# Batch 0's two first products lead, the interleaved streams begin one chunk earlier, and loads of k and v wait for the transposes of k

## Chip, cores and metric

One core of a Trainium2 chip. The metric is the device time of one launch in microseconds (us), lower is better. The profiled span runs from the first to the last instruction of one execution; in these runs it is about 1.8 us less than the launch's own time. Runs come with a state, fast or slow; everything below compares fast runs. The granted clock of a stretch is the share of TensorE's full clock that the profile shows as granted there; the landing of a transfer is the time from its issue until its data is in place; PSUM is the memory that matmuls write to, cut into banks.

## The reference, cut to what matters

```python
# B=8, H=8, S=1024, D=64, KP=64; 8192 tokens, d_model 512, d_ff 2048
k_proj = einsum('ks,bhsd->bhkd', E, k)
v_proj = einsum('ks,bhsd->bhkd', F, v)
scores = (q @ k_proj.T) / sqrt(64)
attn   = exp(scores - max) / sum          # softmax over 64 columns
x      = (attn @ v_proj)  -> 8192 x 512   # heads side by side
h      = maximum(x @ w_in, 0)             # the "first" product, 8192 x 2048
out    = (h * h) @ w_out                  # the "second" product, 8192 x 512
```

## The kernel before

The work is cut into 16 chunks: batch b, half c, 512 tokens each. A chunk's x comes out of attention as `xT`, and then has a first and a second product. Each product is done in one of two ways. **Plain**: 64 matmuls of 512 columns. **Seven**: the operands are cut into 2 by 2 blocks and seven half-size products of sums of blocks take the place of eight (112 matmuls of 256 columns; VectorE makes the sums). Most chunks run in "streams": firsts and seconds, both as seven products, alternate in quanta of four matmuls, 28 steps for a chunk. The attention of later batches is put between the quanta by a plan of step numbers.

```python
def first_plain(self, order=..., sums=True):
    for n, fb in enumerate(order):
        ps = bank()
        for cb in range(NCB):
            self.first_mm(fb, cb, ps)         # 4 matmuls of 512 columns
        self.square(fb, ps)                   # ScalarE relu, VectorE square
        if sums and n % HF == HF - 1:
            self.sum_h(n // HF)
        yield                                 # one step of the plan
# ... second_cold: the plain second product, two banks at a time
# ... second_seven: the same by seven products

def project(self):
    ps = att_psum()[:, 0]
    for i in range(NI):
        f, l = i == 0, i == NI - 1
        nc.tensor.matmul(ps[LO, :], lhsT=ET[:, i, :], rhs=self.K[:, :, i, :], start=f, stop=l)
        nc.tensor.matmul(ps[HI, :], lhsT=FT[:, i, :], rhs=self.V[:, :, i, :], start=f, stop=l)
    # ... copies of k by VectorE, of v by ScalarE and VectorE

def transpose_k_dma(self):
    nc.sync.dma_start_transpose(kT, kp)       # views cut

# weights: four pieces of w_out are loaded last
for j in range(WP):
    if j == WP - 1:
        load(Q0[:, :, 4:8, :], tokens(q, 0, i=slice(4, 8)))   # q of batch 0, second chunk
    # ... load of w_out piece j

# the kernel's start: TensorE is kept busy on zeros while loads arrive
warm(8)
ET = projection("ET", e_bf)
warm(4)
# ... attention of batch 0, first chunk, with warm(1) to warm(3) between

# the order of the products before the streams
run_all(chunk[0, 0].first_cold(), chunk[0, 0].second_cold(), chunk[0, 1].first_plain(),
        chunk[0, 1].second_seven(*(bank()[:] for _ in range(3))))
# ...
run_all(chunk[1, 0].first_plain())
# then the streams: firsts from (1, 1) on, seconds from (1, 0) on
#   with, once a batch, at steps counted by t:
    on(t + 2, b + 2, "transpose_q_dma")
    on(t + 11, b + 3, "load_q", ...)
    on(t + 28, b + 2, "project")
    on(t + 30, b + 2, "transpose_k_dma")
    on(t + 32, b + 3, "load_kv")              # straight behind the transpose
```

The softmax here doesn't subtract the row's maximum and nothing guards it: scores larger than these inputs give would overflow.

## Time and profile before

| | before |
|---|---|
| three runs, us | 479.88, 480.07, 483.85 (median 480.07) |
| profiled span, us (same run timed 480.92) | 479.1 |
| granted TensorE clock | 1.0 |
| TensorE busy / weight loads busy | 98% / 73% |
| VectorE / ScalarE busy | 73% / 60% |
| start of the streams, us | 109.48 |

TensorE is busy all through, so the time is the sum of its columns and its gaps. The lines that show this stand in the prediction. This is TensorE's timeline of the kernel before (start, length, engine, line, operation, tiles, shape, count, and in brackets the idle time before and what ended it):

```profile
6.16 1.89 PE L221 MATMUL ps_bank<-zeros 128*128 128x512 bf16 x4
7.98 1.84 PE L272 MATMUL ps_bank<-K_sb,ET 128*64 128x256 bf16 x8
...
25.12 0.38 PE L494 MATMUL ps_bank<-xT,w_in 128*128 128x512 bf16 x1 [0.16 <-issue]
25.76 0.59 PE L494 MATMUL ps_bank<-xT,w_in 128*128 128x512 bf16 x2 [0.26 <-DVE xT L439]
```

The matmul at 25.76 us is the first one after the last piece of the first chunk's `xT`: from here on TensorE runs freely. I call this moment **the start**, and the span less the start **the rest**: 479.1 - 25.76 = 453.3 us before.

### The profile page before, as it was taken

The page shows a single profiled execution, that of the slowest core. Times are in us where ns is not written, and L with a number is a line of the kernel's source. Part 1 is how long each engine was busy: PE and PEld are TensorE (multiplying, and loading weights), DVE is VectorE, ACT ScalarE, POOL GpSimd, SP SyncE. Part 2 cuts the span into 40 slices and gives each one's busy share as a digit, 9 for nine tenths or more (in the row PEclk, how much of TensorE's full clock was granted, in tenths as well). Part 3 has the DMA queues.
Part 4 walks back from the last instruction along what each step waited for, and adds up shares of the span by engine and source line. Part 5 has one row for each costly group of instructions (what it writes and reads, how often), then busy time and mean ns, then how long its engine had stood idle before and what let it go on. Part 6 is the DMA issues. An engine that isn't in the chain of part 4 may idle for free.

```text
span 479.1 us, 10022 instructions
## 1 busy us (share of the span) xinstructions
PE 469.1 (98%) x4096; PEld 351.9 (73%) x4106; DVE 349.2 (73%) x613; ACT 286.2 (60%) x466; POOL 33.3 (7%) x45
## 2 busy tenths in 40 slices
PE   8999999999999999999999999999999999999996
PEld 3444445637878787887878878787878788888885
DVE  2356898856996679767897579966797678967671
ACT  2564567397547774678546785477736775565641
POOL 7410020200010000100010000100000000000000
PEclk9999999999999999999999999999999999999999
DMA  9999998899949497867949498595911054101012
GB/s 180 204 206 206 227 157 158 158 227 207 178 90 181 111 201 175 127 127 185 185 99 204 89 221 176 93 163 135 212 52 55 23 133 112 67 23 67 24 66 89
DMA packets 80046, 66.98 MB, mean 140 GB/s; under 512 B 30720, under 2 KB 76032, under 8 KB 80000
## 3 DMA queue, kind: packets, MB, share of 16 engines
q0 software_dynamic: 30640, 29.23, 39.3%
q1 hardware_dynamic: 49216, 36.97, 29.8%
q8 instruction: 32, 0.52, 0.5%
q10 hardware_dynamic: 144, 0.13, 0.1%
q14 instruction: 14, 0.11, 0.1%
HBM read 59.24 MB, written 16.78 MB: 159 GB/s over the span
## 4 chain that ended last, share of the span: by engine, by line
PE 86%; DVE 8%; ACT 3%; issue 1%; DMA 1%; DVEq 0%; ACTq 0%
PE ps_bank L657 35%; PE ps_second L577 33%; PE ps_bank L494 6%; PE ps_att L334 2%; PE ps_att L263 2%; PE ps_second L554 2%; PE ps_att L410 2%; DVE rs L378 1%; DVE w_in_sum L155 1%; DVE w_out_sum L155 1%; DVE xT L439 1%; DVE h L155 1%; PE ps_bank L221 1%; DMA e_f<-in_E_dram 1%; ACT h L490 1%
## 5 line engine op out<-in xcount | busy, mean ns | idle before, releaser
L155 DVE TENSOR_TENSOR h<-h 128x1024 bf16<-128x1024 bf16 (+1 forms) x182 | 107.8, 615 | 38.9 <-ACT h L667 25.3
L657 PE MATMUL ps_bank<-x_sum,w_in_sum 128*128 128x256 bf16 x624 | 94.0, 273 | 0.0
L657 PEld LDWEIGHTS <-w_in_sum 128*128 128x128 bf16 x832 | 78.7, 98 | 16.2 <-issue 7.5
L577 PEld LDWEIGHTS <-h 128*128 128x128 bf16 x832 | 81.3, 98 | 10.7 <-issue 1.0
L549 ACT COPY u<-ps_bank 128x512 f32<-128x512 f32 x107 | 63.2, 591 | 24.5 <-PE ps_bank L657 21.4
L671 DVE CUSTOM_DVE_ANT_0 h<-ps_bank,u 128x512 bf16<-128x512 f32 x104 | 68.3, 684 | 13.0 <-PE ps_bank L657 12.5
L682 ACT COPY ps_bank<-ps_bank 128x512 f32<-128x512 f32 x52 | 29.7, 570 | 78.7 <-PE ps_bank L657 78.7
L667 ACT ACTIVATE h<-ps_bank 128x512 bf16<-128x512 f32 x104 | 63.0, 606 | 16.4 <-PE ps_bank L657 15.5
L657 PEld LDWEIGHTS <-w_in 128*128 128x128 bf16 x624 | 58.8, 98 | 13.9 <-issue 7.2
L577 PEld LDWEIGHTS <-s 128*128 128x128 bf16 x624 | 61.0, 98 | 7.1
L657 PE MATMUL ps_bank<-xT,w_in 128*128 128x256 bf16 x416 | 62.6, 273 | 0.0
L577 PE MATMUL ps_second<-w_out_sum,s 128*128 128x256 bf16 x416 | 62.5, 273 | 0.0
L577 PE MATMUL ps_second<-w_out_sum,h 128*128 128x256 bf16 x416 | 62.2, 273 | 0.0
L577 PE MATMUL ps_second<-w_out,h 128*128 128x256 bf16 x416 | 60.1, 272 | 0.1
L414 DVE TENSOR_TENSOR xT<-ps_att,rs 128x512 bf16<-128x512 f32 x56 | 36.0, 684 | 15.9 <-PE ps_att L410 15.9
L494 PE MATMUL ps_bank<-xT,w_in 128*128 128x512 bf16 x186 | 44.6, 379 | 2.1 <-DVE xT L439 1.0
L490 ACT ACTIVATE h<-ps_bank 128x512 bf16<-128x512 f32 x48 | 28.1, 606 | 16.1 <-PE ps_bank L494 15.9
L155 DVE TENSOR_TENSOR o_sb<-ps_second,u 128x512 f32<-128x512 f32 x27 | 18.5, 684 | 25.9 <-PE ps_second L577 20.7
L494 PEld LDWEIGHTS <-w_in 128*128 128x128 bf16 x192 | 17.7, 97 | 24.6 <-issue 6.1
L348 ACT ACTIVATE expT<-ps_att 128x1024 bf16<-128x1024 f32 x32 | 32.9, 1036 | 2.9 <-PE ps_att L334 2.5
L657 PE MATMUL ps_bank<-x_sum,w_in 128*128 128x256 bf16 x208 | 31.3, 273 | 0.0
L657 PE MATMUL ps_bank<-xT,w_in_sum 128*128 128x256 bf16 x208 | 31.3, 273 | 0.0
(104 smaller groups left out, 477.8 us busy)
## 6 DMA issues: line engine op xcount, KB each, us to landing
out_dram<-o_sb SPq DMA_DIRECT2D x63, 256.0 KB, 3.1
rs<-inv SPq DMA_DIRECT2D x96, 128.0 KB, 2.6
K_sb<-in_k_dram POOLq DMA_DIRECT2D x7, 1024.0 KB, 10.7
V_sb<-in_v_dram POOLq DMA_DIRECT2D x7, 1024.0 KB, 17.1
Q_sb<-in_q_dram POOLq DMA_DIRECT2D x7, 1024.0 KB, 12.1
w_out<-in_moe_w_out_dram POOLq DMA_DIRECT2D x4, 512.0 KB, 18.0
w_in<-in_moe_w_in_dram POOLq DMA_DIRECT2D x3, 512.0 KB, 14.9
k_f<-in_k_dram SPq DMA_DIRECT2D x1, 512.0 KB, 4.7
```

Source lines behind the costliest of these rows:

```text
L155: return nc.vector.tensor_tensor(out=o, in0=x, in1=y, op=op)
L263: nc.tensor.matmul(ps[LO, :], lhsT=ET[:, i, :], rhs=self.K[:, :, i, :], start=f, stop=l)
L348: self.done = nc.scalar.activation(e[:], ps[:], AF.Exp, scale=SCALE)
L414: self.done = nc.vector.tensor_tensor(out=self.xT[:, pr, :, par], in0=ps_x[par].rearrange("p (c t) -> p c t", c=2), in1=rs[:, par].rearran ...
L490: nc.scalar.activation(h, ps.rearrange("p (a t) -> p a t", a=2), AF.Relu)
L494: nc.tensor.matmul(ps[:], lhsT=w_in_blk(cb, fb), rhs=self.xT[:, cb, self.c].rearrange("p a t -> p (a t)"), start=(cb == 0), stop=(cb == NC ...
L549: nc.scalar.copy(u[:], ps)
L577: nc.tensor.matmul(ps[:, i * HM:(i + 1) * HM], lhsT=self.h_form(n, fb)[:, i * P:(i + 1) * P], rhs=w_out_form(n, fb), start=fresh and i == ...
L657: nc.tensor.matmul(ps[:, j * HC:(j + 1) * HC], lhsT=w_in_form(n, cb, 2 * self.g + j), rhs=self.chunk.x_form(n, cb), start=fresh and j == 0 ...
L667: nc.scalar.activation(self.out(kh, a), ps[:], AF.Relu)
L671: nc.vector._custom_dve(TENSOR_ADD_SAT, out=self.out(kh, a), in0=ps[:], in1=more[:], s0=3.0e38, s1=0.0)
L682: nc.scalar.copy(self.chain[:], self.first[:])
```

## The change

Its intent: batch 0's two first products lead, so the second product of chunk (0,0) can be done as seven products instead of plainly, and so can the first product of (1,0), which moves into the streams. The attention of batch 0's second chunk and of batch 1 is squeezed in earlier, in half chunks. Six squares go to ScalarE. Loads of k and v wait until the DMA transpose of k has landed. k and v are projected to two PSUM banks. Cut to its core (a new plan of steps, buffer counts and re-timed operand sums, and two copies of transposes that move to ScalarE, are cut; `t` is 28 steps larger after than before for the same `b`, since the streams begin one chunk, 28 steps, earlier):

```diff
-    if j == WP - 1:                                  # before the last w_out piece
-        load(Q0[:, :, 4:8, :], tokens(q, 0, i=slice(4, 8)))
+    if j == 2:                                       # after w_in piece 3 of 5
+        for g in range(2):
+            load(Q0[:, half[g], 4:8, :], tokens(q, 0, h=half[g], i=slice(4, 8)))
...
-            ps = att_psum()[:, 0]
+            ps = att_psum()
-  matmul(ps[LO, :], lhsT=ET ...);  matmul(ps[HI, :], lhsT=FT ...)
+  matmul(ps[LO, 0], lhsT=ET ...);  matmul(ps[HI, 1], lhsT=FT ...)
...
-run_all(chunk[0, 0].first_cold(), chunk[0, 0].second_cold(), chunk[0, 1].first_plain(),
-        chunk[0, 1].second_seven(...))
+run_all(chunk[0, 0].first_cold(),
+        chunk[0, 1].first_plain(sums=False, on_scalar=(1, 4, 7, 10, 12, 14)))
...
-run_all(chunk[1, 0].first_plain())
+run_all(chunk[0, 0].second_seven(*banks))
...                                                   # firsts(): (1, 0) is no longer skipped
-            on(t + 2, b + 2, "transpose_q_dma")
+            on(t + (26 if b else 32), b + 2, "transpose_q_dma")
-            on(t + 32, b + 3, "load_kv")
+            on(t + (32 if b else 37), b + 3, "load_kv", lambda b=b: atts[b + 2].kT_done)
```

## The prediction

> **What bounds the kernel now.** I read the page first (busy shares, then the 40 slices), then TensorE's timeline, the waits by stretch, the DMA queue, and VectorE's and ScalarE's timelines between 15 and 112 us. The page:
>
> ```profile
> PE 469.1 (98%) x4096; PEld 351.9 (73%) x4106; DVE 349.2 (73%) x613; ACT 286.2 (60%) x466; POOL 33.3 (7%) x45
> ...
> PE   8999999999999999999999999999999999999996
> ...
> PEclk9999999999999999999999999999999999999999
> ```
>
> TensorE is busy from end to end at full clock; no other engine passes 73%. So the time is TensorE's columns plus its gaps, and a change gains only by taking matmuls or gaps away. Two rates, from TensorE's timeline (start, length, engine, line, tiles, count, and in brackets the idle time before):
>
> ```profile
> 37.17 4.48 PE L500 MATMUL ps_bank<-w_out,h 128*128 128x512 bf16 x20
> 41.49 1.06 PE L309 MATMUL ps_bank<-ident,Q_sb 128*128 128x128 bf16 x16
> 42.38 1.89 PE L500 MATMUL ps_bank<-w_out,h 128*128 128x512 bf16 x8
> ...
> 118.35 0.41 PE L410 MATMUL ps_att<-expT,vp 64*64 64x512 bf16 x4
> 118.69 0.61 PE L657 MATMUL ps_bank<-x_sum,w_in_sum 128*128 128x256 bf16 x4
> 119.14 0.60 PE L577 MATMUL ps_second<-w_out_sum,s 128*128 128x256 bf16 x4
> ```
>
> Start to start, 20 wide matmuls (512 columns) take 41.49 - 37.17 = 4.32 us, 0.216 each; 16 transposes 0.89 us. Later in that timeline a quantum of four 256-column matmuls starts every 0.437 us (18 of them from 119.14 to 127.00), so 0.1092 each. A group of attention matmuls put between costs 0.43 us: the quantum before 118.35 started at 117.82, should end at 118.26, and the next starts at 118.69. A projection of k and v costs 1.94 (135.32 to 137.26).
>
> Where are the gaps? From 112 to 470 us the waits name nothing for TensorE but weight loads of 0.2 to 0.4 us ("issue"), the transitions that I have counted. In 25 to 112 us they name small ones:
>
> ```profile
> PE ps_bank L554 <- DVE h L155: 0.5, 1, 0.5
> PE ps_bank L494 <- DVE qT L323: 0.3, 1, 0.3
> PE ps_bank L494 <- DVE xT L439: 0.3, 1, 0.3
> ```
>
> All waits of matmuls there sum to about 2 us. The start of the kernel to 25.76 us (last piece of the first xT) is not touched, and the streams from 109.48 us run without a gap. The change can act only between.
>
> **What the Trainium skill says.** "TensorE: Matmul & The Clock Gate", Back-to-back issue gap, gives N/2.4 + 2.5 ns for an isolated warm matmul: 215.8 and 109.2 ns for 512 and 256 columns. The trace agrees (216 and 109). The same place gives about 131 ns as the sustained spacing at 512 columns; this trace does not. "Perfetto Trace Analysis", Identifying the Most-Contended Engine, says matmul busy share is a poor measure of headroom and names weight-load share (73% here) instead. Taken here, headroom is in the number of columns, and that is what the change cuts. "PSUM — Partial Sum Buffer", PSUM bank collisions, says different quadrants of one bank may be accessed at the same time. k lies in partitions 0 to 63 and v in 64 to 127 of one bank before, yet ScalarE's copy of v waited for VectorE's copies of k (0.4 us in two cases), so that wait is one of ordering; separate banks may lift it, off TensorE's path. "DMA: Bandwidth & Descriptors", Queues, rings and completion order, says each DMA engine takes turns between queues by packet. The k transposes took 10.1 us to land in the median, 2.3 at the least, the last one, which has no loads of k and v issued beside it. That agrees with sharing.
>
> **The change part by part.**
>
> (a) Two plain products become seven-product ones: the second product of batch 0's chunk 0, and the first product of batch 1's chunk 0. By the instruction order of both programs, 128 wide matmuls go (192 + 64 to 128) and 224 of 256 columns come (112 in each stream). 128 x 0.216 = 27.65 us out, 224 x 0.1092 = 24.46 in: **-3.2 us**.
>
> (b) Attention is cut into chunk halves for batch 1 as for batch 0, so two pairs no longer share one packed group of sums. By both programs' orders: six more groups of sums for one half each, three packed ones fewer, scores and values in the same number of groups: +3 at 0.43 us, less 0.3 for batch 2's k transposes going to DMA: **+1.0 us**. With (a): -2.2.
>
> Both together by stretch. Before, 25.76 to 109.48 us holds 181 wide matmuls (39.1), the 64 wide second ones (13.8), 112 of 256 (12.2), and 15.2 of attention: 80.4 of 83.7 us, so 3.3 us of gaps. After, from 25.76 to the streams: 117 wide (25.3), 112 of 256 (12.2), 10.8 of attention (six transposes of q at 0.45, five groups each of scores and sums, four of values, one projection 1.94, k transposes): 48.3, so the streams start at 74.1 us plus gaps. Their first 28 steps are new: 28 x 0.873 + 8 groups x 0.43 + 1.94 = 29.8. From step 28 on the plan equals the old one from its step 0, with one more group: 479.1 - 109.5 + 0.4 = 370.0. Sum: **474.0 us plus gaps**, against 479.1 with 3.3 of gaps before. So at equal gaps about -1.8 us (0.4 from the count above: groups that stand beside each other before).
>
> (c) Gaps after. I walked the engines' orders by hand with the trace's durations (ACT relu 0.49 back to back, exp or ln 0.95, DVE square 0.34, copy or sum 0.6, xT 0.63). *Loads:* the queue moves about 206 GB/s (bf16 side) there, 2.55 us for 512 KB:
>
> ```profile
> 21.95 0.75 POOL L89 DMA_DIRECT2D w_out<-in_moe_w_out_dram  x1 [1.44 <-DMA V_sb<-in_v_dram]
> 24.73 0.88 POOL L89 DMA_DIRECT2D K_sb<-in_k_dram  x1 [2.03 <-DMA w_in<-in_moe_w_in_dram]
> 27.25 0.87 POOL L89 DMA_DIRECT2D V_sb<-in_v_dram  x1 [1.63 <-PE ps_bank L494]
> ```
>
> The second line says that w_in's blocks 4 to 7 landed at about 24.7. After, q's halves follow (26.0, 27.3), then blocks 8 to 11 (29.9), 12 to 15 (32.4). TensorE reaches q's halves at 28.4 and 29.8 and block 8 at 31.8: it fits by 2 us. k and v of batch 1 land by about 53, their projection comes at about 57. *Start of the second chunk:* batch 0's chunk-1 attention is squeezed into steps 6 to 14. ScalarE runs exp, ln, exp between relus, and VectorE's last xT comes at about 42.0 where TensorE would want it at 41.2: a gap of **0.8 us**. *Chunk (0,1):* VectorE has 16.9 us of squares, s sums and weight sums to do; w_out's sums end at about 57, product 5 wants them at about 59. ScalarE takes six squares and stays under the matmuls' pace (22 x 0.5 = 11 of 13.8 us). *Second product of (0,0):* exp and ln fill ScalarE almost wholly (10.6 of about 10.5 us in steps 7 to 14), and scores, sums and values hand two PSUM pairs round: a few waits of 0.1 to 0.3, **about 1 us**. *First ten stream steps:* ScalarE still works off exp of 1/sum while the bank copies of the streams begin: **0.5 to 1 us**. The k transposes of batch 2 have 9 steps to their scores, some 10.6 us from the start of the projection; the copies take about 5, and with loads held back the transpose should take 2.3 to 5. It just fits. Gaps: about 2.5 to 3, so span 474.0 + 2.8 = 476.8.
>
> (d) Holding loads of k and v behind the transposes costs nothing later: the next projection is over 40 us away, a load takes 5 us at the rate above. The separate banks cost and save nothing on TensorE. The change of the h and x_sum buffers (nine shared) moves one x_sum to just before its use; VectorE has room.
>
> **Rivals.** *First: nothing is lost on the way, and the denser order removes the old gaps too.* For it: the old waits of matmuls stem from sums and copies that are moved. Against: the work of ScalarE and VectorE per us of matmul rises in 25 to 75 us. It would give 474 to 475. *Second: a new wait in the thick part takes back the 1.8 us and more.* Candidates: ScalarE, where before one four-us stretch already ran nearly full (4.72 of 5 us in 45 to 50); q or w_in landing late, if 1 KB runs of q move slower than my rate; the k transposes of batch 2 against their nine steps, where every us of delay is a us of time. For it: three margins of about 2 us each. Against: none falls short by the sums above. It would give 479 to 485. *Third: the gain is larger in the steady part, because transposes land earlier.* Against: TensorE has no wait on kT from 112 us on (transposes issued at 140.45 landed about 150.8, scores ran at 151.51). It would give nothing.
>
> **Range and chances.** The measured time before is 1 us over the profiled span (480.07 and 479.1), so 476.8 + 0.9 = 477.7; I round to 477.5. Low end 474 (gaps near zero), high end 482 (one of the three margins fails by 3 to 4 us). Over 2% faster means under 470.5, less than TensorE's bare columns by my sum: 0.02. Over 2% slower means above 489.7, at least 12 us of new gaps: 0.04, for a transfer that collides in a way I did not see. Within 2%: 0.94.
>
> **What would show it.** In TensorE's timeline after: start of the streams at 75 to 78 us (my sum 74.1 plus gaps of 1 to 3); first part to 25.76 us the same; 28 steps later about 30 us on; then the same 55.5 us for each batch. Waits of matmuls should name xT at the second chunk's start (near 41 us), ScalarE's copies or exp between 58 and 85 us. The k transposes' median landing should fall from 10.1 to under 5 us. I am wrong if a wait on kT, qT, w_in or q of over 2 us stands in TensorE's list, if a batch in the streams takes more or less than 55.5 us by 0.5, or if the streams start before 74 us.

## The result, and the profile after

| | before | after |
|---|---|---|
| median, us (four runs each) | 479.99 (479.88 to 483.85) | 475.57 (475.43 to 475.9) |
| ratio of fast runs, 95% interval | | 0.989 [0.984, 0.9939]: within 2% |
| profiled span, us (own time) | 479.1 (480.92) | 473.7 (475.5) |
| granted clock | 1.0 | 1.0 |
| start / rest, us | 25.76 / 453.3 | 24.04 / 449.7 |

A ratio here is the mean time of one kernel's fast runs over that of the other's of the same rounds, so it is not quite the ratio of the medians quoted. The page of the changed kernel:

```profile
PE 465.2 (98%) x4224; PEld 361.3 (76%) x4230; DVE 348.3 (74%) x606; ACT 296.1 (63%) x482; POOL 33.9 (7%) x47
...
PE   8899999999999999999999999999999999999996
...
PEclk9999999999999999999999999999999999999999
```

There are 128 more matmul records on TensorE, but 3.9 us less busy time (469.1 to 465.2), at the same clock. TensorE is still the bound. Its timeline at the start, and where the parts of the change begin:

```profile
5.80 1.04 PE L222 MATMUL ps_bank<-zeros 128*128 128x512 bf16 x4
7.07 1.03 PE L278 MATMUL ps_bank<-K_sb,ET 128*64 128x256 bf16 x8 [0.23 <-ACT K_sb L726]
...
37.30 2.33 PE L504 MATMUL ps_bank<-xT,w_in 128*128 128x512 bf16 x9
39.81 0.38 PE L504 MATMUL ps_bank<-xT,w_in 128*128 128x512 bf16 x1 [0.17 <-DVE xT L446]
40.41 13.33 PE L504 MATMUL ps_bank<-xT,w_in 128*128 128x512 bf16 x60 [0.22 <-DVE xT L446]
53.57 1.91 PE L564 MATMUL ps_bank<-w_out,h 128*128 128x256 bf16 x16
...
73.45 0.60 PE L667 MATMUL ps_bank<-xT,w_in 128*128 128x256 bf16 x4
...
102.66 0.60 PE L667 MATMUL ps_bank<-xT,w_in 128*128 128x256 bf16 x4
```

The first two lines are the same work as the first two of the timeline before: there four wide matmuls on zeros took 1.89 us (with the 128x256 ones, 1.84, still half as fast), here 1.04. The clock was open by about 6 us here, and at about 9.5 us before. The other lines are the landmarks. The second chunk starts at 37.30 (two of its 72 wide matmuls, up to 53.57, have no record here); two small waits for `xT` at 39.8 and 40.4; the second product of (0,0) as seven products starts at 53.57; the streams start at 73.45; 28 steps later it is 102.66. The whole list of waits of TensorE's matmuls from 24 us to the end is one line (us in total, times, longest; one of the three, 0.26 us, ends at the start itself):

```profile
PE ps_bank L504 <- DVE xT L446: 0.7, 3, 0.3
```

And the transposes of k by DMA, before (first fence) and after (second), the view of the tile `kT`:

```profile
L300 SPq DMA_TRANSPOSE kT<-kp x5: 1210/1269/1336, 140.5 to 362.6; - x5
...
DMA to landing us min/median/max: 2.3/10.1/10.3
```

```profile
L306 SPq DMA_TRANSPOSE kT<-kp x6: 1195/1203/1233, 85.3 to 357.2; - x6
...
DMA to landing us min/median/max: 2.3/2.3/2.9
```

The median landing falls from 10.1 to 2.3 us, once no load of k and v is issued beside it.

**Where the 5.4 us of span came from.** The start is 1.72 us earlier, and the rest is 3.6 us shorter. The rest can be added up from the landmarks. The bare work is the prediction's count; that of the remainder is the same stretch as measured in the kernel before, plus one group, so its gap is only a difference to that kernel.

| stretch after | measured, us | bare work, us | gaps, us |
|---|---|---|---|
| start to streams | 73.45 - 24.04 = 49.41 | 48.3 | 1.1 |
| first 28 steps | 102.66 - 73.45 = 29.21 | 29.8 - 0.87 = 28.9 | 0.3 |
| the remainder | 473.7 - 102.66 = 371.04 | 370.0 + 0.87 = 370.9 | 0.2 |
| sum | 449.7 | 448.1 | 1.55 |

The 0.87 are two quanta of 0.437 us that I had put among the first 28 steps and that fall after them, because step 0 has no second product yet and the first group's last product comes late. The bare work before was 80.4 us up to the streams and 479.1 - 109.48 = 369.6 from there, 450.0 in all, with 3.3 of gaps. So the bare work fell by 1.9 and the gaps by 1.75. The gaps are what the count leaves over, so an error of the count would stand in them. The lists of waits say about the same: after the start they name 2.0 us before (2.3 from 25 us on, less the 0.26 that end at 25.76) and 0.4 after, 1.6 less.

### The profile page after: what moved, and what is told of

It reads as the page before. It is cut to its first block, busy times and chain, and to the rows that moved or that the text cites.

```text
span 473.7 us, 10305 instructions
## 1 busy us (share of the span) xinstructions
PE 465.2 (98%) x4224; PEld 361.3 (76%) x4230; DVE 348.3 (74%) x606; ACT 296.1 (63%) x482; POOL 33.9 (7%) x47
## 4 chain that ended last, share of the span: by engine, by line
PE 89%; DVE 4%; DMA 3%; ACT 2%; SPq 1%; issue 1%; DVEq 0%; ACTq 0%
PE ps_bank L667 35%; PE ps_second L587 34%; PE ps_bank L504 4%; PE ps_bank L564 3%; PE ps_att L269 2%; PE ps_att L341 2%; PE ps_second L564 2%; DMA rs<-inv 2%; PE ps_att L417 2%; DMA k_f<-in_k_dram 1%; PE ps_att L394 1%; DVE xT L446 1%; PE ps_bank L316 1%; DVE h L156 1%; DVE xT L421 1%
## 5 line engine op out<-in xcount | busy, mean ns | idle before, releaser
L667 PE MATMUL ps_bank<-x_sum,w_in_sum 128*128 128x256 bf16 x672 | 101.2, 273 | 0.0
L667 PEld LDWEIGHTS <-w_in_sum 128*128 128x128 bf16 x896 | 84.3, 98 | 18.8 <-issue 9.6
L587 PEld LDWEIGHTS <-h 128*128 128x128 bf16 x896 | 87.6, 98 | 11.4 <-issue 1.1
L681 DVE CUSTOM_DVE_ANT_0 h<-ps_bank,u 128x512 bf16<-128x512 f32 x112 | 73.9, 685 | 16.9 <-PE ps_bank L667 12.7
L559 ACT COPY u<-ps_bank 128x512 f32<-128x512 f32 x115 | 68.0, 591 | 25.5 <-PE ps_bank L667 24.0
L677 ACT ACTIVATE h<-ps_bank 128x512 bf16<-128x512 f32 x112 | 67.9, 607 | 16.7 <-PE ps_bank L667 15.8
L667 PE MATMUL ps_bank<-xT,w_in 128*128 128x256 bf16 x448 | 67.4, 273 | 0.0
L421 DVE TENSOR_TENSOR xT<-ps_att,rs 128x512 bf16<-128x512 f32 x48 | 30.9, 685 | 14.1 <-PE ps_att L417 14.1
L587 PE MATMUL ps_second<-w_out,s 128*128 128x256 bf16 x224 | 33.6, 273 | 0.0
L504 PE MATMUL ps_bank<-xT,w_in 128*128 128x512 bf16 x124 | 29.9, 379 | 1.8 <-DVE xT L446 1.5
L504 PEld LDWEIGHTS <-w_in 128*128 128x128 bf16 x128 | 11.8, 98 | 16.8 <-issue 4.4
## 6 DMA issues: line engine op xcount, KB each, us to landing
K_sb<-in_k_dram POOLq DMA_DIRECT2D x7, 1024.0 KB, 10.3
Q_sb<-in_q_dram POOLq DMA_DIRECT2D x6, 1024.0 KB, 11.8
```

The lines of the kernel that those rows point to most:

```text
L421: self.done = nc.vector.tensor_tensor(out=self.xT[:, pr, :, par], in0=ps_x[par].rearrange("p (c t) -> p c t", c=2), in1=rs[:, par].rearran ...
L504: nc.tensor.matmul(ps[:], lhsT=w_in_blk(cb, fb), rhs=self.xT[:, cb, self.c].rearrange("p a t -> p (a t)"), start=(cb == 0), stop=(cb == NC ...
L559: nc.scalar.copy(u[:], ps)
L587: nc.tensor.matmul(ps[:, i * HM:(i + 1) * HM], lhsT=self.h_form(n, fb)[:, i * P:(i + 1) * P], rhs=w_out_form(n, fb), start=fresh and i == ...
L667: nc.tensor.matmul(ps[:, j * HC:(j + 1) * HC], lhsT=w_in_form(n, cb, 2 * self.g + j), rhs=self.chunk.x_form(n, cb), start=fresh and j == 0 ...
L677: nc.scalar.activation(self.out(kh, a), ps[:], AF.Relu)
```

## The experiments

Twelve runs in three groups, each on one chip with its own runs of the kernel before. Where a difference of less than one us matters, I compare the rest of one profile with that of another, because the time itself contains the start, which varies (see a_again). The rest of a given kernel repeats within about 0.6 us: 453.3, 453.9 and 453.5 for the kernel before, 449.7, 449.9 and 449.5 for the changed one (the last of each with a longer warm-up).

### 1. a_again: the changed kernel, unaltered

> The changed kernel unaltered, as the control of this group. Of the 5.4 us between the two profiled spans, 1.7 lie ahead of the first matmul of the first xT (25.76 against 24.04 us), which the change does not touch. If that is the phase of TensorE's clock warming up, this profile may show a start anywhere between 24 and 26 us, and the time stays near 475.6 us. If the change itself makes the start shorter, the start is again at 24.0.

Measured: median 477.51 us (477.07 to 479.43), ratio 0.9945 [0.9928, 0.9963]: half the gain of the first result has gone. TensorE's timeline:

```profile
5.83 1.89 PE L222 MATMUL ps_bank<-zeros 128*128 128x512 bf16 x4
7.65 1.87 PE L278 MATMUL ps_bank<-K_sb,ET 128*64 128x256 bf16 x8
...
25.46 0.81 PE L504 MATMUL ps_bank<-xT,w_in 128*128 128x512 bf16 x3 [0.26 <-DVE xT L446]
...
74.87 0.60 PE L667 MATMUL ps_bank<-xT,w_in 128*128 128x256 bf16 x4
```

Here the zeros take 1.89 us as in the kernel before, and the start is at 25.46, not 24.04. The span is 475.4, so the rest is 449.9. The rest is a property of the kernel, the start is not: the same kernel, same code, gave 24.04 and 25.46. "TensorE: Matmul & The Clock Gate" of the Trainium skill, Part 1, says that the clock gate watches a free-running window of about 3.4 us and that the number of cold matmuls therefore varies from run to run; the traces agree in that the number varies: four wide matmuls took 1.04 us at 5.80 and 1.89 at 5.83, at about half the rate. The window itself shows in no run here.

### 2. b_again: the kernel before, unaltered

> The kernel before, unaltered, for a second profile of its start. If the start of 25.76 us is one of two phases of the clock's warm-up, this one may show 24 to 26; if the kernel before always starts late, 25.8 again. Time 480 us either way.

Measured: 480.56 us (479.36 to 481.61), ratio 1.0011 [0.999, 1.0032]; start 25.85, span 479.7, rest 453.9. The kernel before repeats as well; it merely starts late in both profiles.

### 3. e8_warm10_after and e9_warm10_before: a longer warm-up in both

```diff
-        warm(8)
+        warm(10)
         ET = projection("ET", e_bf)
```

> The changed kernel with ten in place of eight matmuls on zeros at the very start, which fill the gap of 0.4 to 0.7 us ahead of the first transposes. Over ten profiles, the start (first matmul after the last xT) lay between 24.0 and 26.2 us for the same instructions, the late ones with half-speed matmuls until about 9.5 us. Theory: the gap decides whether TensorE's clock opens at 5 or 9.5 us. Then the start is 24.0 to 24.8 in every run, the median 475 and the spread under 1 us (it was 477.07 to 479.43 in one group and 475.43 to 475.9 in another). Rival (the late start is the loads): median and spread as before, 475.5 to 479.

> The kernel before with the same ten matmuls. Theory: 0.5 to 1.5 us faster than the kernel before, 478.5 to 479.3, and from the start to the end still 453.6 us. Against the changed kernel with ten it then shows what the change itself is worth without the luck of the clock: 3.8 us.

Measured in one group: e8 475.44 us (475.17 to 476.59), ratio 0.9898 [0.988, 0.9916], start 23.86, rest 449.5; e9 479.96 us (479.51 to 480.21), ratio 0.9988 [0.9972, 1.0003], start 24.34, rest 453.5. The kernel before ran from 479.44 to 481.63 in this group, 2.2 us wide; e9 is 0.7 wide. The medians differ by 4.5 us; of the 4.4 between the two profiled spans, 0.5 is the start and 3.9 the rest. With the start nearly alike in the two profiles, **the change is worth about 4 us**. The half us was there before the first projection began (6.90 and 7.35 us): from there to the start it takes 16.96 us in e8, 16.99 in e9 and 16.97 in the first profile of the changed kernel, so the change itself does not shorten the start. The three profiles with ten matmuls on zeros (e8, e9, e10) start at 23.86 to 24.34, the eleven with eight at 24.03 to 26.21; that fits the theory, but three profiles do not prove it. Not all was met: e8's start lay under its 24.0 and its spread was 1.4 us, not under 1, and e9's median lay above its 479.3. Whether the longer warm-up gains time is not shown: e9 is like its kernel within the noise, and no unaltered run of the changed kernel stands in this group (475.44 here, 475.57 and 477.51 in others).

### 4. e1_one_bank: v projected to the bank of k again

```diff
-                nc.tensor.matmul(ps[HI, 1], lhsT=FT[:, i, :], rhs=self.V[:, :, i, :], start=f, stop=l)
+                nc.tensor.matmul(ps[HI, 0], lhsT=FT[:, i, :], rhs=self.V[:, :, i, :], start=f, stop=l)
...
-            self.keep_v(ps[HI, 1])
+            self.keep_v(ps[HI, 0])
```

> k and v projected to one PSUM bank again, all else as changed. My theory (the gain is columns of TensorE and fewer gaps): no difference to the changed kernel, under 0.3 us. Rival (separate banks save a wait of TensorE or of the k copies): 1 us or more slower.

Measured: 475.85 us, ratio 0.991 [0.9893, 0.9927]; rest 449.6 against 449.9 of a_again on the same chip. The separate banks are worth nothing on the time. (Its median is 1.7 us under a_again's with nothing better in the rest. Its profiled start was 24.82 against 25.46; there the clock opened early, but TensorE waited 1.01 us for ScalarE's copy of the first k, and in e4 0.52 us for a load of k, so a late operand can move the start too. ScalarE's copy of v still waits for VectorE's copies of k, 1.2 us in five cases with two banks and 1.1 with one, so the banks do not lift that wait either. For the other runs only the times are known.)

### 5. e3_plain_second: the second product of (0,0) plain again

```diff
-        at(18, chunk[0, 0].sum_h, 0)
-        at(20, chunk[0, 0].sum_h, 1)
...
-        run_all(chunk[0, 0].second_seven(*banks))
+        run_all(chunk[0, 0].second_plain(banks))   # 4 token blocks, 16 wide matmuls each
```

> The second product of batch 0, chunk 0 is done plainly again (64 wide matmuls in place of 112 of 256 columns), in 16 steps at the same place. My theory: 64 x 0.216 - 112 x 0.1092 = 1.6 us slower than the changed kernel, perhaps up to 0.3 less since VectorE is spared eight sums. Rival (columns are not what counts, the gaps are): no slower, since VectorE has 4.8 us less to do.

Measured: 478.44 us, ratio 0.9957 [0.9942, 0.9973]; rest 451.2, so +1.3 against a_again. TensorE's timeline:

```profile
38.63 15.83 PE L504 MATMUL ps_bank<-xT,w_in 128*128 128x512 bf16 x72
54.30 1.03 PE L510 MATMUL ps_bank<-w_out,h 128*128 128x512 bf16 x4
...
76.61 0.60 PE L676 MATMUL ps_bank<-xT,w_in 128*128 128x256 bf16 x4 [0.67 <-ACT o_sb L517]
```

From the product's start to the streams it takes 76.61 - 54.30 = 22.31 us; in a_again 74.87 - 54.98 = 19.89. Of the 2.42 us, 0.67 is a wait for a copy of the result that the experiment itself brings in. The other 1.75 fits 64 x 0.216 - 112 x 0.1092 = 1.6: the gain of columns for one product stands at the place where it was expected. The rest grew by 1.3 only, because e3 saves about 0.6 us before this stretch and 0.5 after it (a_again has a wait of 0.4 there for a second-product bank). As to the first of these, the small waits for `xT` at the second chunk's start are gone: 72 matmuls in one run from 38.63, most likely because VectorE was spared the sums of h for (0,0), the only work that this edit takes from it there.

### 6. e4_q_late: the second half of batch 0's q loaded late again

```diff
-        if j == 2:
-            for g in range(2): load(Q0[:, half[g], 4:8, :], ...)
...
+        if j == WP - 1:            # before the last piece of w_out
+            for g in range(2): load(Q0[:, half[g], 4:8, :], ...)
```

> The second half of batch 0's q is loaded behind three quarters of w_out, where the kernel before had it, all else as changed. My theory: it lands near 39.6 us as it did before, TensorE wants it at 26.8, so 12 to 13 us of wait, plus up to 2 us of slow clock after it: 12 to 15 us slower than the changed kernel. Rival (order of loads does not matter, the queue has room): under 2 us.

Measured: 489.67 us (487.93 to 490.09), ratio 1.0193 [1.0173, 1.0214]; rest 463.5, +13.5 to 13.9 against the three profiles of the changed kernel. TensorE's timeline:

```profile
38.20 1.03 PE L316 MATMUL ps_bank<-ident,Q_sb 128*128 128x128 bf16 x8 [10.43 <-DMA Q_sb<-in_q_dram]
39.03 1.91 PE L504 MATMUL ps_bank<-xT,w_in 128*128 128x512 bf16 x4
```

A wait of 10.43 us, and after it four wide matmuls in 1.91 us, where they take 1.03 at full clock. The granted clock over the stretches (start and end; width, then busy time and count of each engine, the clock, the DMA share, GB/s):

```profile
27.00:37.00 10.00, 0.77 (x4) 0.15 (x2) 1.12 (x3) 1.39 (x3) 1.76 (x2) 0.77 1.27 204
37.00:41.00 4.00, 2.80 (x15) 1.70 (x16) 1.02 (x2) 0.02 (x1) 0.00 (x0) 0.50 1.31 204
41.00:60.00 19.00, 18.61 (x116) 7.64 (x114) 14.48 (x32) 16.13 (x25) 1.75 (x2) 0.96 1.05 163
```

By stretches of one us, the clock fell to 0.50 during the wait, between 32 and 33 us, and rose again between 42 and 43. So TensorE worked some 4.4 us, from 38.2 to about 42.6, at half rate, which loses about 2.2. Two later waits for ScalarE, of 1.0 us (a logarithm, explained under e7) and 0.2, complete the sum: 10.4 + 2.2 + 1.2 = 13.8. Moving this load is what makes the new order possible; it is not a gain but a condition.

### 7. e2_loads_free: k and v loaded without waiting for the transpose

```diff
-  on(t + (32 if b else 37), b + 3, "load_kv", lambda b=b: atts[b + 2].kT_done)
+  on(t + (32 if b else 37), b + 3, "load_kv")
```

> Loads of k and v no longer wait for the transposes of k. My theory: the k transposes land 10.3 us after issue in place of 2.3, so batch 2's, issued at 85.3, lands at 95.6 and its scores, at 91.4 us now, wait about 4.2 us; later batches have 16 steps and lose under 0.5 in all: 4 to 5 us slower than the changed kernel. Rival (the transposes were late for another cause): landing stays at 2.3, no difference.

Measured: seven runs from 485.74 to 503.46 us, median 492.37; ratio of the fast runs 1.019 [1.015, 1.0231]. Three of the seven, the profiled one among them (503.46 us, clock 0.98), were classed slow, by their times against the fastest of this kernel. No other kernel here spreads as wide (17.7 us), so the class may have taken up part of the effect itself. Four fast runs have a mean of 489.6, against 477.8 for a_again in the group: **+12 us, where I expected 4 to 5**. In the profile, TensorE's waits and the landing of `kT`:

```profile
PE ps_att L341 <- DMA kT<-kp: 17.7, 4, 6.1
```

```profile
DMA to landing us min/median/max: 2.4/13.4/15.5
```

And its timeline at the longest wait:

```profile
99.72 0.64 PE L341 MATMUL ps_att<-qT,kT 64*64 64x512 bf16 x4 [6.12 <-DMA kT<-kp]
100.30 1.04 PE L667 MATMUL ps_bank<-x_sum,w_in_sum 128*128 128x256 bf16 x4
101.12 1.06 PE L587 MATMUL ps_second<-w_out_sum,h 128*128 128x256 bf16 x4
```

Two things were missed. The landing got worse than in the kernel before (13.4 against 10.1), so four batches waited and not one. And after such a wait quanta that take 0.60 us take 1.04; the granted clock from 100 to 104 us was 0.58. The sizes of single waits come from a profile classed slow and are not those of the fast runs; that it costs over 10 us not to hold the loads, with everything else as changed, the fast runs show alone.

### 8. e7_free_q_early: loads free, and the transposes and loads of q at their old steps

```diff
-  on(t + (26 if b else 32), b + 2, "transpose_q_dma")
+  on(t + (2 if b else 32), b + 2, "transpose_q_dma")
...                                  # load_q of batch b + 3 back at t + 11; e2's edit kept
```

> As e2 (loads of k and v free), and from batch 3 on the transposes and loads of q are back where the kernel before had them, 24 steps earlier than the transposes of k. e2 lost far more than I expected: its k transposes landed after 13.4 us in the median, not 10.3, and four batches waited. Theory: the q transposes issued just ahead on the same queue add the missing 3 us. Then landing falls to about 10.3 from batch 3 on, only batch 2 waits (some 6 us and 2 to 3 of slow clock after it): 8 to 10 us slower than the changed kernel, some 485. Rival (something else makes the landing long): 13 us still, as slow as e2, some 492.

Measured: 480.13 us (479.83 to 482.42), ratio 1.0002 [0.9981, 1.0024]; rest 452.5. The view of `kT` and the waits of TensorE's matmuls:

```profile
DMA to landing us min/median/max: 2.3/9.9/10.0
```

```profile
PE ps_att L417 <- ACT inv L398: 2.9, 1, 2.9
```

The landing goes back from 13.4 to 9.9, the 10.1 of the kernel before. So the excess of e2 comes from the transposes of q that the change puts four steps ahead of those of k, on the same queue; the 10 us come from the loads. (This run moves the loads of q with them. But in e2 itself, beside loads, the four k transposes that took 11.8 to 15.5 us were issued while the q transpose was still in flight, as at 145.4 us with q landing at 148.7; the one at 206.5, issued after q had landed at 205.3, took 10.3.) No matmul waits for `kT` any more. I expected about 485 because I thought batch 2 would still wait. It did not: batch 3's loads of k and v came only at 89.6 us, behind a load of q, and the transpose was issued at 86.8, so that it could land in the 2.3 us that it takes alone. The loss in the rest against the changed kernel (2.8 us; of the 4.7 us in time against e8 a further 1.8 is the start, 25.71 against 23.86) is one wait for a logarithm on ScalarE, which itself sat idle until 113.33 us. The profile names a store of the output as what it waited for, but another transfer fits better. By the code the logarithm writes a buffer from a pool of three, which one `inv` and two `rs` tiles take in turn, so the copies `rs<-inv` out of the `inv` before must have landed first. The last of these was issued at 106.6 and took 6.7 us, so it landed at 113.3. In the changed kernel the last was issued at 105.4, took 2.8 us, and nothing waited. The shorter waits of the same name in e4 (1.0 us) and e10 (0.5 us) end in the same way: the last copies were issued at 118.4 and 104.7 and took 4.8 and 4.3, and the logarithms started at 123.2 and 109.1. What was slow in e7 is likely the queue: its edit brings a load of q from 114.9 to 88.8 us, ahead of those of k and v, and the load of v lands 22.3 us after its issue instead of 14.3. So the loads need not be held as such: with the transposes of q early, letting them go cost this one wait in the profile.

### 9. e5_dve_squares: all squares of (0,1) on VectorE

```diff
-  chunk[0, 1].first_plain(sums=False, on_scalar=(1, 4, 7, 10, 12, 14))
+  chunk[0, 1].first_plain(sums=False, on_scalar=())
```

> All squares of batch 0, chunk 1 on VectorE again. It gets 6 x 0.34 = 2.0 us more in a stretch where it runs without a break from 38 to 57 us. w_out's first sums then end 1.5 us later, still before product 5 (57.3 us), and the copies of k end at 60.9 where TensorE transposes k at 60.3: 0.3 to 1 us slower. Rival (VectorE has room there): no difference; second rival (VectorE is the bound there): 2 us slower.

Measured: 476.31 us, ratio 0.9925 [0.9906, 0.9943]; rest 450.4, +0.5 to 0.9. The waits of its matmuls are those of a_again (1.0 us for `xT`, 0.4 for ScalarE's copy of a second-product bank), so none of them is put down to the squares; the difference is as large as the spread of the rest between runs of one kernel. The six squares on ScalarE are worth under 1 us, and that they are worth anything is not shown.

### 10. e6_two_banks_first: the second chunk's first matmuls spread over two banks

```diff
+            ahead = {}
+            if on_scalar:                       # only (0, 1)
+                for fb in order[:2]:
+                    ahead[fb] = bank()
+                    for cb in range(2):         # column blocks whose xT is there
+                        self.first_mm(fb, cb, ahead[fb])
             for n, fb in enumerate(order):
-                ps = bank()
-                for cb in range(NCB):
+                ps = ahead[fb] if fb in ahead else bank()
+                for cb in range(2 if fb in ahead else 0, NCB):
```

> A try to beat both: the second chunk of batch 0 begins with the first two blocks of xT for two output banks, so that its third and fourth block are wanted 0.43 us later each. The gaps at 39.2 to 40.4 us are 0.95 us in the trace of the changed kernel. My theory: most of it goes, 0.6 to 0.9 us faster. Rival (the gap moves on to the next wait): no difference.

Measured: 475.24 us (474.85 to 477.46), ratio 0.9911 [0.989, 0.9931]; rest 449.5, 0.2 under the changed kernel's. TensorE's timeline:

```profile
37.30 15.99 PE L504 MATMUL ps_bank<-xT,w_in 128*128 128x512 bf16 x72
53.13 1.91 PE L570 MATMUL ps_bank<-w_out,h 128*128 128x256 bf16 x16
```

The second product starts at 53.13 instead of 53.57, from the same 37.30: 0.44 us saved. At the end 0.2 is left, with a wait of 0.4 us for ScalarE's copy of a second-product bank, which a_again has too and the first profile of the changed kernel has not. The expected 0.6 to 0.9 did not come.

### 11. e10_both: two banks first and the longer warm-up

This is e6's edit and e8's together, the version that might beat both kernels.

> Ten matmuls at the start and two banks first at the second chunk, a try at a version that beats both. From the start to the end 449.3 us as in the run with two banks first; time 474.5 us, 0.3 us under the changed kernel with ten. Rival: no gain beyond the warm start.

Measured: 475.31 us (474.77 to 475.74), ratio 0.9892 [0.9873, 0.9911]; rest 449.7, with a wait of 0.5 us for ScalarE's logarithm. It is not better than e8 (475.44 in the same group) or the changed kernel beyond the noise. No version here beats the change.

## Why the prediction was right, and which terms were not

The range held: 475.57 lies between 474 and 482, 1.9 us under the 477.5. The repeat of the same kernel, a_again, came to 477.51; that this hits the middle value is luck, since two errors cancel in it (below). The mechanism was right; the sizes, step by step:

- **Columns, -3.2 us: right.** Of the two products the one that could be undone alone (e3) gave 1.75 us where half the sum, 1.6, was expected. The other, the first product of (1,0), was not undone; its half stands on the count.
- **Attention in half chunks, +1.0 us: consistent, not shown alone.** Bare work after adds up to 448.1 us with it, and 1.55 us of gaps fill the measured 449.7.
- **Gaps, 2.8 us: the term that was mis-sized.** Measured 1.55 us, a little over half. By place: the start of the second chunk was right in place, releaser and size. It has 53.57 - 37.30 - 72 x 0.216 = 0.7 us against 0.8, by `xT` on VectorE, at 39.8 and 40.4 us. The second product of (0,0) was to have about 1 us of waits for ScalarE and PSUM pairs; no such wait stands in the list, and what is left of the stretch's 1.1 us is 0.4. The first steps of the streams were to have 0.5 to 1; they have 0.3. In both places I had called out ScalarE as nearly full, and in the first profile of the changed kernel no matmul waited for it; a_again has a single such wait, of 0.4 us, and it is in the streams. The first rival (denser order, no new gaps, 474 to 475) came nearer; the third, a gain in the steady part, gave nothing, as the prediction had argued: the remainder differs by 0.2.
- **The start, "not touched": wrong as a statement about a run.** The instructions there are the same in effect, yet the start moved from 25.76 to 24.04 because the clock opened earlier, and the rest of the kernel moved with it. It is chance as far as the change goes: 25.46 in a_again, 23.86 to 26.2 over all profiles. So of the first result's 5.4 us of span, 1.7 are not the change's. For the same reason one test that I set failed by its letter: the streams began at 73.45, before 74 us. Counted from the start, 49.4 us was measured and 74.1 - 25.76 + 2 = 50.3 to be expected with 2 us of gaps.
- **From span to time, +0.9 us: mis-sized.** I took a median of runs less the span of another run. The profiled run itself took 480.92, 1.8 us over its span. The two errors of the middle value go opposite ways: 1.8 for 0.9 raises it, while 1.25 us fewer gaps and a start 1.7 us earlier lower it: 477.7 + 0.9 - 1.25 - 1.7 = 475.65, and 475.57 was measured.
- **Loads fit: right.** No wait for w_in or q stands in the list. The margin for q was 1.4 us, not 2, in that profile: its halves landed at 25.4 and 26.7 us and their transposes ran at 26.8 and 28.1, since the early start brings the need forward and not the loads. e4 shows what it costs when q is late, 13.7 us.
- **k transposes under 5 us: right** (2.3 in the median), and the 9 steps of batch 2 sufficed. The explanation, loads beside them, was half of it: e7 confirms 10 us with the loads, e2 shows that transposes of q just ahead add more.
- **Holding the loads costs nothing: right.** No matmul waits for k or v. **Separate banks are worth nothing on TensorE: right** (e1); that they might lift ScalarE's wait for VectorE's copies of k was not (1.2 us with two banks, 1.1 with one). "PSUM — Partial Sum Buffer" of the skill, PSUM bank collisions, is in line with it: matmuls may write the two halves in one bank, and time does not tell the banks apart.
- **A batch of 55.5 us: right.** Four batches from one DMA transpose of k to the next take (357.2 - 134.96) / 4 = 55.6 us in the changed kernel, and (362.6 - 140.5) / 4 = 55.5 before.

On the skill: the place on the most-contended engine names, besides the weight-load share, the share of peak arithmetic, which the prediction left out.

What stays open: the share of the clock and of the waits in the fast runs of e2; how much of the 1.55 us is gaps and how much an error of the count, since the waits named come to 0.4; and what sets the moment at which the clock opens at the start.

## What to carry to other kernels

Where one engine is busy from end to end, count what it has to do by kind and by measured rate, and put gaps in by place; here the count was right to a few tenths of a us and the guess at gaps nearly twice too high. Before a difference of one per cent is explained, align the traces at the first moment from which work flows freely, since what lies before it may be chance as large as the effect. When an order is made denser, every wait for a transfer that it shortens the distance to must be counted with the clock that it takes away afterwards: 10.4 us of waiting cost about 2.2 more in half-rate work.

## What the Trainium skill lacked or had wrong

- "TensorE: Matmul & The Clock Gate", Back-to-back issue gap: it gives about 131 ns as the sustained spacing at 512 columns. Here 20 in a row take 216 ns each, at a granted clock of 1.0; its formula for an isolated warm matmul (215.8) is what holds, and so does the 215.7 ns that Part 1 of the same page gives for back-to-back matmuls.
- The same page, Part 1: it says that the ramp costs under 1% of a typical span and need not be fitted. That holds in size (the start varied from 23.86 to 26.2 us, 0.5% of the span), but 2.3 us is over half of the 4 us to be measured here, and the page does not say that traces have to be aligned for it.
- The same page, HAM oscillation, works the cost out for repeated waits of 3 to 5 us, with 1.67 us throttled after each. After the single wait of 10.4 us here TensorE worked at a clock of 0.50 for about 4.4 us, and some 2.2 us were lost.
- "DMA: Bandwidth & Descriptors": bandwidths for DMA transposes, but no time to landing of a single one from SBUF to SBUF, nor what loads beside it add. Here it was 2.3 us alone, 10 us beside loads of k and v, and 13.4 us with a transpose of q just ahead on the same queue as well (the last in a profile classed slow).
- "TensorE: Matmul & The Clock Gate", Part 3, has the span of matmuls packed into the array by themselves, but no page that I found gives the cost of a group of 64-row attention matmuls put between full ones: 0.43 us for four of 512 columns here.
